# New order tables for all five engines of a two-layer linear-attention and SwiGLU kernel

## Chip, core and metric

The kernel runs on one core of one Trainium2 chip. The metric is device time in microseconds (us) of one execution. A core has TensorE (PE in the profile; PEld is its weight load), VectorE (DVE), ScalarE (ACT), GpSimd (POOL) and SyncE (SP), each with an instruction stream of its own; here SP issues every DMA.

## The reference

x is 2048 x 512 in float32. The same weights are used in both layers.

```python
def _A_ref(x, wqkv, wo):           # linear attention, H = 32 heads of 16
    q, k, v = ...                  # x @ wqkv, split by head
    phi = lambda t: jnp.where(t > 0, t + 1, jnp.exp(t)) + 1e-6
    pq, pk = phi(q), phi(k)
    kv = jnp.einsum("bhsd,bhse->bhde", pk, v)
    z = jnp.einsum("bhsd->bhd", pk)
    num = jnp.einsum("bhqd,bhde->bhqe", pq, kv)
    den = jnp.einsum("bhqd,bhd->bhq", pq, z)[..., None] + 1e-6
    return ... @ wo                # (num / den), heads joined

def _B_ref(x, w1, w3, w2):         # F = 1792
    return (silu(x @ w1) * (x @ w3)) @ w2

x = x + _A_ref(_layernorm(x), A_wqkv, A_wo)
x = x + _B_ref(_layernorm(x), B_w1, B_w3, B_w2)
x = x + _A_ref(_layernorm(x), A_wqkv, A_wo)
x = x + _B_ref(_layernorm(x), B_w1, B_w3, B_w2)
```

## The kernel before, in words

**Numbers.** Every float32 operand of a product is split into two float16 parts, a high one and a low one (the rest). `mm` (L878) makes each product as three matmuls (high by high, low by high, high by low; `PASSES`), each accumulating in a bank of PSUM.

**Attention.** The 2048 rows are 16 tiles of 128. Per tile t, `ln_moments` (L840, L841, VectorE) makes mean and variance; `ln_scale` makes the scale and the offset with four small GpSimd instructions: L848, the power of -1/2 (L849), L851, L852. `normalise` (L855, ScalarE) writes the normalised row. For a key tile, `keys_turn` makes the high part (L790 on ScalarE or L792 on GpSimd) and the low part (L1497, VectorE or GpSimd), and SP transposes both by DMA (L1498; L870 for the first three tiles). Then TensorE makes pk, the key product of 12 matmuls of 512 columns. phi of it is ScalarE's L1228 to L1230 and VectorE's L1239, and its parts are L1306 (ScalarE) and L1321 (VectorE). The sums over rows for the denominators are matmuls into pz (L1261) or adds on GpSimd (L1312). The Gram product gt takes 12 matmuls per key tile. The transposed tile is stored (`keep_transposed`, L1515) and read back for the queries (`load_query`, L1528). Weights for later come in meanwhile: x tiles L1977, attention weights L1982, blocks of w1 and w3 L893.

**MLP.** Rows go in four chunks of 512 (`mlp_rows`: transposes L1629 and L1637, store of the chunk L1641, reload L1813, 1792 KB each), the hidden width in seven groups of 256. Each group's first product has seven half-size products, P1 to P7, in place of eight. They go into three PSUM banks, ba, bb and bc. bb is copied to SBUF by ScalarE (L1692), and VectorE adds ba and bc (L1695), after which the next product may overwrite the bank. silu is L1647, times the second product L1648, and the parts of the hidden rows are L1651 and L1653. The second product goes into po: `mlp_out` (L1739), or at some places `mlp_out_plain` (L1759). `mlp_add` adds po to the rows in SBUF (L1788 on VectorE, then L1808 and L1809 on GpSimd; L1775 on VectorE after the plain form), and `store_row` (L1769) sends rows to the output. Prepared groups of weights are kept in DRAM (stores L1111, fetches L1120).

**What sets the order.** Each engine runs its own instructions strictly in its stream's order, and an instruction waits there for what it needs from others. The function `arrange` at the end of the trace takes, for each engine, a string of the table `ORDER`: the traced instructions' numbers in the order in which they are to stand. It makes each instruction depend on the one that the string puts ahead of it, without any semaphore (`tc.add_manual_dep(..., NoSync)`), so the tables fix all five streams and nothing else does. A number is the instruction's place in the order in which the program text issues it. SP's stream has a second rule: its DMAs take eight semaphores in turn, so a DMA waits for the landing of the one eight places ahead.

The program's own text already has an order of work (the strings `KEYS`, `FIRST`, `TURN`, `HOOKS`), and a table of which engine does each movable operation (`ENGINES`). The tables come from a planner outside the file that gives every instruction a duration; only its results, the strings, are in the kernel.

Of the kernel before, what the change touches and what calls it, by code (L numbers as in the profile page):

```python
# [73 lines left out]
        "0-56 59-61 57-58 62-64 71-82 65-67 85-87 68-70 94-108 91-93 83-84 109-113 117-119 88-90 "  # L74
        "114-116 123-134 137-139 149-160 120-122 143-145 140-142 135-136 161-172 146-148 184-186 "
        "175-177 181-183 207-212 173-174 187-198 201-203 178-180 204-206 199-200 213-226 230-232 "
        "239-250 227-229 233-235 265 251-252 266 259-261 256-258 284-286 253-255 236-238 267-280 "
        "262-264 281-283 290-292 287-289 293-304 313-315 305-306 319-330 316-318 310-312 331-332 "
        "339-341 345-356 342-344 307-309 333-335 368-370 336-338 371-382 365-367 357-358 392-394 "
        "359-361 389-391 395-396 418-420 397-408 383-385 409-411 421 362-364 386-388 422-424 "  # L80
        "412-417 431-433 428-430 446 425-427 437-439 434-436 443-445 440-442 447-570 583-594 "
        "571-582 595-762 775-786 763-774 787-883 908-913 920-925 884-895 932-943 896-907 926-931 "
        "914-919 956-973 980-991 1016-1027 944-949 1124 974-979 1125 950-955 992-1003 1028-1033 "
        "1126 1034-1039 1127 1064-1069 1128-1130 1004-1009 1131-1135 1010-1015 1136-1137 1140 "
        "1138-1139 1388 1100-1105 1389-1390 1106-1111 1391 1144 1392 1145 1393 1052-1057 1394 "
        "1146-1147 1395-1396 1141-1142 1397 1040-1045 1398-1402 1070-1075 1403 1046-1051 "
        "1408-1409 1404-1406 1410-1411 1407 1143 1058-1063 1232 1412 1233-1235 1076-1081 1413 "
        "1082-1087 1112-1123 1172-1177 1414-1415 1088-1099 1236 1416 1237-1249 1178-1183 1252 "
        "1250 1253-1254 1417-1418 1251 1419 1428 1148-1153 1208-1213 1160-1171 1154-1159 "
        "1420-1423 1340-1343 1424 1220-1225 1214-1219 1280-1285 1255 1184-1189 1425 1190-1195 "  # L90
        "1316-1321 1426 1344-1345 1322-1327 1286-1291 1346 1348 1196-1201 1226-1231 1347 "
        "1349-1354 1356 1202-1207 1355 1357-1362 1429 1427 1432 1430 1433-1435 1363 1256-1261 "
        "1431 1436 1262-1267 1437 1444 1438 1268-1273 1439-1443 1445-1446 1274-1279 1447-1459 "
        "1292-1297 1328-1333 1298-1303 1460-1471 1304-1315 1496-1501 1334-1339 1520-1537 "
        "1502-1504 1538 1376-1381 1540-1542 1364-1369 1382-1387 1784 1370-1375 1785 1539 1543 "
        "1786 1508-1513 1628-1630 1505-1507 1631 1472-1477 1514-1519 1787-1788 1478-1483 "
        "1568-1573 1789-1791 1632 1636 1574-1579 1484-1495 1633-1635 1637-1643 1648 1644-1647 "
        "1649 1792-1793 1604-1609 1794-1798 1556-1561 1544-1555 1562-1567 1610-1615 1799-1805 "
        "1736 1808 1616-1621 1809 1580-1585 1737-1738 1586-1591 1676-1681 1739 1650 1622-1627 "
        "1810 1651 1811 1592-1603 1740 1806-1807 1741-1757 1812 1652-1657 1682-1687 1813-1816 "  # L100
        "1658-1663 1817-1821 1712-1717 1822 1664-1669 1823 1670-1675 1824-1830 1718-1723 1832 "
        "1831 1833-1835 1688-1693 1836-1837 1840 1838-1839 1841-1843 1694-1699 1844-1845 1848 "
        "1846 1758-1759 1847 1849-1851 1724-1729 1852-1854 1856-1861 1855 1700-1705 1862-1867 "
        "1892-1897 1706-1711 1730-1735 1916-1917 1920-1921 1924-1925 1918-1919 1760-1765 "
        "1772-1777 1928 1778-1783 1930 1929 1766-1771 1922-1923 1931-1932 1926-1927 1934 "
        "1868-1873 1898-1903 1874-1879 1904-1909 2021-2022 1910-1915 1933 1936 1935 1880-1891 "
        "1961-1972 2023-2026 1937-1942 1997-2002 2029-2030 2027-2028 2031-2032 2035-2036 "
        "2039-2040 2003-2008 2037 1949-1960 1973-1978 1943-1948 1979-1984 2038 2009-2014 "
        "2033-2034 1985-1990 2066-2071 2102-2107 2015-2020 2041 2138-2139 2134-2135 1991-1996 "
        "2126-2127 2072-2077 2136-2137 2042-2047 2128-2131 2140 2132-2133 2144-2146 2141 "  # L110
        "2108-2113 2054-2065 2048-2053 2114-2119 2142 2120-2125 2078-2083 2171-2172 2143 "
        "2173-2174 2234-2241 2185 2084-2089 2186 2175-2178 2187-2188 2196-2197 2192-2193 "
        "2179-2182 2189-2190 2194 2183-2184 2090-2101 2191 2195 2200-2201 2198-2199 2202-2209 "
        "2213-2214 2210-2211 2221 2159-2164 2147-2152 2217-2218 2153-2158 2219-2220 2165-2170 "
        "2222 2215-2216 2212 2223-2226 2229 2242-2245 2270-2275 2230-2233 2276-2281 2227-2228 "
        "2282-2287 2339-2340 2294-2295 2341-2343 2246-2251 2298-2299 2296-2297 2252-2257 "
        "2302-2305 2300-2301 2308 2312 2306-2307 2313 2258-2263 2288-2293 2310 2314 2344-2345 "
        "2264-2269 2309 2311 2399-2400 2375-2380 2315-2320 2381-2386 2327-2338 2321-2326 "
        "2401-2404 2411-2412 2346-2350 2405-2410 2387-2392 2413 2444-2449 2414-2418 2504-2505 "
        "2351-2362 2480-2485 2393-2398 2419 2363-2374 2486-2491 2450-2455 2506-2511 2516-2518 "  # L120
        "2512-2515 2519-2524 2432-2437 2420-2425 2438-2443 2549-2552 2563-2564 2570-2571 "
        "2426-2431 2572-2573 2584-2585 2553-2554 2591-2592 2456-2461 2593-2594 2605-2606 "
        "2462-2467 2555-2556 2565-2566 2574-2577 2586-2587 2557-2562 2567 2492-2497 2568-2569 "
        "2582-2583 2595-2596 2578-2581 2588-2590 2597-2598 2468-2473 2599-2600 2498-2503 "
        "2672-2673 2474-2479 2601-2602 2607 2603-2604 2609-2611 2525-2530 2612-2621 2648 "
        "2537-2548 2622-2623 2531-2536 2649-2653 2608 2674-2675 2660-2665 2654-2659 2624-2629 "
        "2666-2671 2676-2677 2630-2635 2680-2683 2678-2679 2684-2686 2688 2690 2687 2717-2722 "
        "2689 2777-2778 2636-2641 2691 2723-2727 2642-2647 2753-2758 2692 2779-2782 2693-2698 "
        "2785-2788 2728 2789-2790 2705-2710 2797 2711-2716 2795 2791 2783-2784 2792-2793 2796 "
# [1963 lines left out]
```

## Time and profile before

| what | us |
|---|---|
| three runs: median (lowest to highest) | 1154.07 (1153.33 to 1154.54) |
| the profiled run, whole | 1151.51 |
| its span, from the first to the last instruction | 1149.8 |
| TensorE busy in it | 1139.5 |
| VectorE, ScalarE, GpSimd busy | 822.0, 628.8, 405.8 |
| first key product of layer 0 starts | 11.93 |

The profiled execution is one run of its own; 1.7 us of its time lie outside the span. The stages can be told by the lines on TensorE: keys of layer 0 up to about 105 us, queries and output of the attention to 188, the first MLP to about 590 while the keys of layer 1 begin at about 575, the second attention to 755, the second MLP to the end.

A row of the timeline reads: start, length, engine, line, operation, output and inputs, count; in brackets how long the engine was idle ahead of it, and what released it. Rows of the same operation that follow one another are drawn together. In the list of waits a row has the waiting engine and line, what released it, then the total in us, the number of times and the longest. Matmuls are pipelined, so a row of x12 is longer by one matmul's passage than its twelve issues.

### The profile page before, as it was taken

How to read it: one execution, taken by the hardware profiler on the slowest of the kernel's cores; microseconds unless marked ns; L12 is line 12 of the kernel's file. 1: busy time of each engine (PE TensorE's matmuls, PEld its weight loads, DVE VectorE, ACT ScalarE, POOL GpSimd, SP SyncE). 2: the span in 40 equal slices, each digit the busy share in tenths (PEclk: the TensorE clock that was granted, in tenths of full speed). 3: DMA queues.
4: the chain of work that ended last, by engine and by line, in shares of the span. 5: the costliest groups of instructions: out<-in, count | busy, mean ns of one | idle time of the engine just before them, and what ended most of it. 6: DMA issues, size and time to landing. Idle time of an engine off the chain costs nothing.

```text
span 1149.8 us, 21802 instructions
## 1 busy us (share of the span) xinstructions
PE 1139.5 (99%) x8862; PEld 864.0 (75%) x8862; DVE 822.0 (71%) x1401; ACT 628.8 (55%) x1078; POOL 405.8 (35%) x472
## 2 busy tenths in 40 slices
PE   8999999999999999999999999999999999999998
PEld 3445445888888888888854454478888888888887
DVE  6888888977878986778774467847866676556533
ACT  6587878866544554334457644776554434343422
POOL 4533688411101312212568615771153110303111
PEclk9999999999999999999999999999999999999999
DMA  9975666875854221111314715674253440022001
GB/s 277 316 231 201 183 171 129 229 170 180 242 203 182 99 84 65 65 65 66 92 32 128 216 41 122 120 172 93 77 134 116 169 174 1 28 80 101 1 19 56
DMA packets 163397, 147.43 MB, mean 128 GB/s; under 512 B 129632, under 2 KB 138976, under 8 KB 158688
## 3 DMA queue, kind: packets, MB, share of 16 engines
q1 hardware_dynamic: 163296, 146.04, 44.3%
q8 instruction: 69, 1.13, 0.4%
q14 instruction: 32, 0.26, 0.1%
HBM read 72.48 MB, written 42.07 MB: 100 GB/s over the span
## 4 chain that ended last, share of the span: by engine, by line
PE 94%; POOL 3%; DMA 1%; DVE 1%; ACT 1%; issue 0%; SPq 0%; POOLq 0%
PE bb L878 25%; PE po L1739 18%; PE bc L878 13%; PE pq L878 7%; PE po L878 7%; PE ba L878 6%; PE gt L878 6%; PE pk L878 5%; PE po L1759 4%; DMA arena<-arena 1%; DMA arena<-in_A_x_dram 1%; POOL arena L1312 0%; PE kv L878 0%; PE pm L878 0%; PE pz L1261 0%; POOL rs_all L849 0%
## 5 line engine op out<-in xcount | busy, mean ns | idle before, releaser
L878 PEld LDWEIGHTS <-arena 128*128 128x128 f16 x6360 | 617.8, 98 | 242.5 <-DMA arena<-arena 6.6
L878 PE MATMUL bb<-arena 128*128 128x256 f16 x2688 | 348.7, 273 | 0.1
L1739 PE MATMUL po<-arena 128*128 128x256 f16 x1932 | 266.7, 273 | 0.0
L1692 ACT ACTIVATE arena<-bb 128x512 f32<-128x512 f32 x196 | 115.8, 593 | 226.0 <-PE bb L878 186.5
L1739 PEld LDWEIGHTS <-arena 128*128 128x128 f16 x1932 | 189.0, 98 | 22.3
L878 PE MATMUL bc<-arena 128*128 128x256 f16 x1344 | 178.9, 273 | 0.0
L1695 DVE TENSOR_TENSOR arena<-arena,bc 128x512 f32<-128x512 f32 x112 | 76.7, 685 | 102.5 <-PE bc L878 56.6
L1653 DVE TENSOR_TENSOR arena<-arena 128x512 f16<-128x512 f32 (+1 forms) x90 | 104.4, 1162 | 32.1 <-ACT arena L1651 32.1
L1647 ACT ACTIVATE arena<-arena,scalars 128x512 f32<-128x512 f32 (+1 forms) x112 | 74.5, 666 | 96.2 <-DVE arena L1695 87.0
L1651 ACT ACTIVATE arena<-arena 128x512 f16<-128x512 f32 (+1 forms) x112 | 98.9, 886 | 33.5 <-DVE arena L1666 13.1
L1788 DVE SCALAR_TENSOR_TENSOR arena<-po,scalars,arena 128x256 f32<-128x256 f32 (+1 forms) x170 | 94.6, 584 | 27.5 <-PE po L1739 18.9
L1648 DVE SCALAR_TENSOR_TENSOR arena<-arena,scalars 128x512 f32<-128x512 f32 (+1 forms) x112 | 80.9, 723 | 39.4 <-ACT arena L1647 38.0
L878 PE MATMUL ba<-arena 128*128 128x256 f16 x672 | 92.1, 273 | 0.0
L878 PE MATMUL pk<-arena 128*128 128x512 f16 x384 | 87.8, 379 | 3.3 <-DMA arena<-arena 3.3
L878 PE MATMUL gt<-arena 128*128 128x512 f16 x384 | 88.9, 379 | 0.8 <-ACT arena L1306 0.6
L878 PE MATMUL pq<-arena 128*128 128x512 f16 x384 | 86.6, 379 | 0.0
L878 PE MATMUL po<-arena 128*128 128x512 f16 x384 | 86.5, 379 | 0.0
L1808 POOL TENSOR_TENSOR arena<-arena 128x512 f32<-128x512 f32 x25 | 34.1, 1366 | 114.7 <-DVE arena L1788 114.7
L1653 POOL TENSOR_TENSOR arena<-arena 128x512 f16<-128x512 f32 x22 | 27.0, 1225 | 124.2 <-ACT arena L1651 84.5
L1809 POOL TENSOR_TENSOR arena<-arena 128x512 f32<-128x512 f32 x25 | 37.0, 1479 | 84.0 <-DVE arena L1788 83.9
L1759 PE MATMUL po<-arena 128*128 128x256 f16 x480 | 64.8, 273 | 0.0
L855 ACT ACTIVATE arena<-arena,nb_all,rs_all 128x512 f32<-128x512 f32 x64 | 51.0, 805 | 17.4 <-POOL nb_all L852 14.4
(163 smaller groups left out, 1286.1 us busy)
## 6 DMA issues: line engine op xcount, KB each, us to landing
arena<-xb_d SPq DMA_DIRECT2D x12, 1792.0 KB, 7.7
xb_d<-arena SPq DMA_DIRECT2D x8, 1792.0 KB, 7.5
xt_d<-arena SPq DMA_DIRECT2D x32, 256.0 KB, 3.3
arena<-xt_d SPq DMA_DIRECT2D x32, 256.0 KB, 3.1
arena<-in_B_w_dram SPq DMA_DIRECT2D x8, 896.0 KB, 6.6
arena<-in_B_w_dram SPq DMA_DIRECT2D x28, 256.0 KB, 3.1
w_d<-arena SPq DMA_DIRECT2D x4, 1792.0 KB, 9.5
arena<-w_d SPq DMA_DIRECT2D x4, 1792.0 KB, 7.4
```

What stands on the lines that cost most here:

```text
L855: nc.scalar.activation(dst, x_sb[:, t, :], AF.Identity, scale=rs_all[:, t : t + 1], bias=nb_all[:, t : t + 1],)
L878: nc.tensor.matmul(dst, lhs(a, k), rhs(b, k), start=first and k == 0 and i == 0, stop=last and k == n - 1 and i == len(PASSES) - 1, skip_g ...
L1647: nc.scalar.activation(t, gate, AF.Silu, scale=info["u1"])
L1648: nc.vector.scalar_tensor_tensor(t, up, info["hid"], t, OP.mult, OP.mult)
L1651: nc.scalar.activation(hs[:, 0, lo:hi], t[:, lo:hi], AF.Copy)
L1653: engine.tensor_tensor(hs[:, 1, lo:hi], t[:, lo:hi], hs[:, 0, lo:hi], OP.subtract)
L1692: nc.scalar.activation(dst, bank_, AF.Copy)
L1695: nc.vector.tensor_tensor(dst, dst, bank_, OP.add)
L1739: nc.tensor.matmul(po[:, i * HALF : (i + 1) * HALF], hs[:, a, qx, cs], w2[:, b, qw, :], start=g == ends[0] and i + a + b == 0, stop=g == e ...
L1759: nc.tensor.matmul(acc[n][:, half * HALF : (half + 1) * HALF], hs[:, a, qx, cs], w2_a21[g][:, b] if (i, half) == (0, 1) else w2[:, b, i + ...
L1788: nc.vector.scalar_tensor_tensor(dst, src, cb, to, OP.mult, OP.add)
L1809: engine.tensor_tensor(x1, x1, u[:, 1:], OP.add)
```

## The change

Only the strings in `ORDER` differ; every other line is the same, though 16 lines lower, as the new strings take 16 lines more (L1769 of the kernel before is L1785 after). The words that come with it: all engines' tables are chosen anew, the planner gives each transfer more room, and it no longer keeps VectorE out of the time of GpSimd's power operation (L849).

In the same place as before stand 1840 of TensorE's 8845 numbers, 313 of VectorE's 1369, 319 of ScalarE's 1025, 181 of GpSimd's 470 and 75 of SP's 326. No number moves to another engine. The largest moves are 93 places forward and 89 back on TensorE, 45 and 155 on VectorE, 42 and 51 on ScalarE, 15 and 24 on GpSimd, 31 and 18 on SP. The beginnings and ends of the strings:

```diff
     "PE": (
-        "0-56 59-61 57-58 62-64 71-82 65-67 85-87 68-70 94-108 91-93 83-84 109-113 117-119 88-90 "
+        "0-56 59-61 57-58 62-64 71-82 65-70 94-108 123-134 88-90 85-87 83-84 109-113 135-136 "
...
-        "8833-8837 8832 8838-8844"
+        "8827-8831 8833 8832 8834-8844"
     "DVE": (
-        "1 6-15 17 16 18 5 19 28 21 20 29 26 30 27 22-25 33 36 34 37 31 43-44 35 45 38-40 52-53 "
+        "1 6-7 5 8-10 12 11 13-15 17 16 18-19 28 20 29 21 33 22-24 34 25-26 30 27 31 36-37 43 45 "
...
-        "1348 1345 1336 1346 1353-1354 1356 1347 1355 1357 1359 1351 1350 1358 1352 1360-1368"
+        "1362 1361 1363-1366 1368 1367"
     "Activation": (
-        "0-13 15 14 17 16 19 18 21-23 20 25 24 26 28 27 30 29 32 34 33 35-36 38 31 41 39-40 42-43 "
+        "0-12 14 13 15 17 19-20 16 18 21 23 22 25 24 26 28 27 30 29 31-32 34 33 41 38 35-36 40 39 "
...
     "Pool": (
-        "6-7 9 8 10 13 11 0 12 14-15 1-2 16-17 19 18 20-21 24 22 28 26 23 31-32 25 27 29-30 33-35 "
+        "6-7 9 8 10-15 0-2 16-17 19 18 20 22 24 23 21 28 26 25 30 27 29 31-35 37 39-40 45 36 42 "
...
     "SP": (
-        "0-7 30 21 8 11-12 9 22 10 26 19 18 25 24 23 20 17 29 13 28 27 38 15 41 31 33 32 39 34-35 "
-        "44 47 37 40 46 42 45 48 36 54 43 53 50 49 51-52 55 63 56-57 14 59 58 61 60 62 16 64 66 "
+        "0-2 4 3 5-6 21 7-8 11 10 9 12 26 19 29 18 30 20 22-24 17 27 45 28 25 13 31 33 32 44 41 "
+        "34-36 46 37 14 39 15 43 42 53 38 81 40 48 47 54 16 51 63 58 49 52 66 50 56-57 55 59 "
...
-        "276 275 277-284 297 286-289 285 291 290 292-294 302 299 296 298 295 301 304 300 307 "
-        "305-306 309-311 308 303 312 314 313 315-325"
+        "272 274-279 281-284 280 285-290 297 292 291 294 293 299 296 302 300 295 303 298 307 "
+        "305-306 309-310 308 311-312 314-315 313 301 316-320 304 321-325"
```

In SP's strings, the numbers 8, 9, 18, 23 and 27 are the transposes of key tiles 0 to 4 of layer 0; 30 is the load of x tile 9; 19, 20, 24 and 28 are stores of transposed tiles; 22, 25 and 29 are blocks of w1. On TensorE, 33-44, 45-56, 71-82, 97-108 and 123-134 are the key products pk of tiles 0 to 4; 65-70, 85-87 and 94-96 are parts of gt of the earlier tiles. The numbers 1367 and 1368 of VectorE are the last two adds of L1775, and 324 and 325 of SP the last two stores of rows (L1769): 324 sends the rows that 1367 writes, 325 those of 1368.

692 rows, old and new, of the table ORDER are left out of this document.

## The prediction

> **What bounds the kernel now.** I read the page's first part, then the list of what PE waited for, then busy time by stretch. The clock stayed at full speed ("clock 1.000"), so it drops out.
>
> ```profile
> span 1149.8 us, 21802 instructions
> ...
> PE 1139.5 (99%) x8862; PEld 864.0 (75%) x8862; DVE 822.0 (71%) x1401; ACT 628.8 (55%) x1078; POOL 405.8 (35%) x472
> ```
> ```profile
> core 0: 1149.8 us, clock 1.000
> ```
> ```profile
> PE pk L878 <- DMA arena<-arena: 3.3, 4, 1.4
> PE pm_k L739 <- POOL arena masks.py:199: 1.2, 1, 1.2
> PE warm L2006 <- DVE ones L663: 1.1, 1, 1.1
> PE gt L878 <- ACT arena L1306: 0.6, 1, 0.6
> PE gt L878 <- DVE arena L1321: 0.2, 1, 0.2
> ```
> ```profile
> 0.00:27.50 27.50, 22.14 (x90) 8.89 (x90) 17.13 (x44) 17.43 (x27) 12.72 (x35) 1.00 0.98 268
> ...
> 188.00:575.00 387.00, 386.93 (x3512) 343.50 (x3511) 313.29 (x527) 204.20 (x343) 99.61 (x96) 1.00 0.44 133
> ...
> 595.00:625.00 30.00, 28.98 (x134) 12.93 (x133) 14.28 (x26) 20.07 (x32) 27.51 (x45) 1.00 0.37 88
> ...
> 755.00:1135.00 380.00, 380.00 (x3462) 338.54 (x3460) 227.72 (x347) 174.39 (x273) 90.99 (x86) 1.00 0.28 87
> 1135.00:1150.00 15.00, 10.99 (x101) 9.60 (x99) 6.19 (x8) 2.37 (x4) 1.16 (x1) 1.00 0.19 71
> ```
>
> The columns behind the span are busy time (and instructions) of PE, PEld, DVE, ACT and POOL, then clock, DMA share and GB/s. PE is busy 386.93 of 387 us and 380 of 380 us in the two MLPs. Nothing that another engine does there can be seen in the time unless it makes PE wait. All that an order can win is in three places: the start (the list's waits for pk's transposes and for gt), one wait at the layer turn (1.02 us missing in 595:625), and the end (the last 15 us, with 10.99 of PE). The matmuls before the first keys (warm, pm_k) only fill time.
>
> **The change part by part.** No instruction is added or removed. PE keeps 8845 matmuls, VectorE 1369, ScalarE 1026, GpSimd 470 instructions and SP 326 DMAs; only their order on each engine differs. So the sum holds only pauses of PE gained and lost, and the end.
>
> *The start.* PE's pauses behind the first key products, and the DMA that ends them:
>
> ```profile
> 11.93 5.60 PE L878 MATMUL pk<-arena 128*128 128x512 f16 x24 [0.43 <-DMA arena<-arena]
> ...
> 18.13 0.59 PE L878 MATMUL gt<-arena 128*128 128x512 f16 x2 [0.61 <-ACT arena L1306]
> ...
> 21.82 2.76 PE L878 MATMUL pk<-arena 128*128 128x512 f16 x12 [1.45 <-DMA arena<-arena]
> ...
> 27.55 2.76 PE L878 MATMUL pk<-arena 128*128 128x512 f16 x12 [0.37 <-DMA arena<-arena]
> ```
> ```profile
> 22.30 5.20 DMA arena<-arena
> ```
>
> The transposes of tiles 0 to 3 are released behind a saturated DMA (share 0.98, 268 GB/s). SP's new table sends the x tile of position 30 (256 KB) behind the third transpose instead of ahead of the first, so every one of the first three has 256 KB less in front of it. At 268 GB/s that is 0.98 us, the upper end; I take 0.57 us for tile 2, because the tile also overlaps computing and its share of that time is not all on the path. In before, tile 3's transpose stood in SP's queue behind a store that waited for tile 2's transpose (it issued at 22.30, just after tile 2's products began at 21.82). In the new table that store (position 24) stands behind the transpose (23), which only needs the low part of tile 3, whose VectorE instruction is also earlier. Tile 4's cast, low part and transpose come some five to seven places earlier, and its products follow tile 3's directly. What is late next is tile 4: I expect it about 2.5 us behind tile 3, where 2.76 us of tile 3's products cover it. **Gain 0.55 us**: the 1.45 us pause shrinks by 0.57, and the 0.37 us pause stays in about its size, as three gt matmuls (85-87) less stand in front of tile 3's products. Bounds: both shrink fully, 0.57 + 0.37 = 0.94; or tile 4's cover is short by as much as one saturated 256 KB transfer, 0.98, which loses 0.98 - 0.55, about 0.4.
>
> *The power operation.* The old plan kept VectorE and GpSimd's power operation (L849) apart; the new one lets them lie together. Where they met anyway:
>
> ```profile
> 18.11 0.75 DVE L1321 SCALAR_TENSOR_TENSOR arena<-arena,scalars 128x512 f16<-128x512 f32 x1 [0.19 <-ACT arena L1306]
> 18.12 0.55 POOL L849 TENSOR_TENSOR rs_all<-ve,minus_half 128x1 f32<-128x1 f32 x1
> ```
> ```profile
> L1321 DVE SCALAR_TENSOR_TENSOR arena<-arena,scalars x32: 734/752/1693, 18.1 to 660.0; 128x512 f16<-128x512 f32 x32
> ```
> ```profile
> L849 POOL TENSOR_TENSOR rs_all<-ve,minus_half x29: 542/556/1095, 5.0 to 640.9; 128x1 f32<-128x1 f32 x28, 128x4 f32<-128x4 f32 x1
> ```
>
> VectorE's instruction took 0.75 us, its median (min/median/max 734/752/1693), through the whole 0.55 us of the power beside it. The power itself reaches 1095 ns at worst, so if either pays, it is GpSimd. Cost 0; bounds 0 and the 0.54 us more that GpSimd paid at worst, once on the way to a key. The Trainium skill (GPSIMD Engine Reference, section 1, Specifications) says that GpSimd's SBUF interfaces are shared with VectorE, with contention for VectorE instructions that have two SBUF inputs; L1321 is one, and this trace shows no time lost on VectorE's side. By that rule VectorE could be held for each power's time; that is the fifth case below.
>
> *The layer turn.* The wait is for tile 9's transpose, and GpSimd made it late:
>
> ```profile
> 617.57 1.27 POOL L1312 TENSOR_TENSOR arena<-arena 128x512 f32<-128x512 f32 x1
> 618.79 0.55 POOL L849 TENSOR_TENSOR rs_all<-ve,minus_half 128x1 f32<-128x1 f32 x1
> ...
> 619.84 1.16 POOL L1497 TENSOR_TENSOR arena<-arena 128x512 f16<-128x512 f32 x1
> ```
> ```profile
> 621.68 1.46 PE L878 MATMUL gt<-arena 128*128 128x512 f16 x6
> 624.16 2.76 PE L878 MATMUL pk<-arena 128*128 128x512 f16 x12 [1.02 <-DMA arena<-arena]
> ```
> ```profile
> 621.03 3.09 DMA arena<-arena
> ```
>
> GpSimd is busy 27.51 of 30 us there. The key's low part (L1497) sits behind an add (L1312, 1.27) of the denominators' sums, which has no early consumer. The new GpSimd table puts low parts ahead of these adds. The transpose at 621.03 starts as the low part ends (619.84 + 1.16 = 621.00). One L1312 out of its way makes it 1.27 us earlier; more than one goes by over the stretch, and walking the new order with these durations lands tile 9 at about 619.3. PE's six gt matmuls issue 0.216 us apart (1.46 = 5 x 0.216 + 0.38), so PE was free at 621.68 + 6 x 0.216 = 622.98 and lost 1.18 us. **Gain 1.2 us**; the pk of tiles 7 and 8 also move 1 to 2 us back in PE's order, which gives their transposes more time. Bounds: 1.2, or 0 if the adds that now come late hold the power operations of the next tiles instead (each 1.27).
>
> *The MLPs.* No pause of PE is there to win except 0.07 us (386.93 of 387); a copy that comes late costs. The leads are short:
>
> ```profile
> 420.55 0.60 ACT L1692 ACTIVATE arena<-bb 128x512 f32<-128x512 f32 x1 [1.49 <-PE bb L878]
> ```
> ```profile
> 421.22 0.82 PE L878 MATMUL bb<-arena 128*128 128x256 f16 x6
> ```
> ```profile
> L1692 ACT ACTIVATE arena<-bb 128x512 f32<-128x512 f32 x196 | 115.8, 593 | 226.0 <-PE bb L878 186.5
> ```
>
> This copy ended at 421.15 and the matmuls that overwrite its bank began at 421.22. There are 196 of them, but ScalarE stood idle 226 us ahead of them, mostly waiting for the matmuls themselves, so a copy normally starts when its product is done, in either order. The new order keeps each copy next to its product where I compared them (408 to 424). I take **0.1 us lost**; bounds 0.2 won, 1.5 lost (three copies, each behind another ScalarE instruction of about its own 0.6 us length).
>
> Of the transfers, one turns late: a 1792 KB reload (L1813), before issued at 316.50, now stands behind the fetch that waits for PE until 327.53.
>
> ```profile
> 296.95 5.91 SPq L1629 DMA_TRANSPOSE arena<-arena  x1
> ...
> 316.50 0.34 SPq L1813 DMA_DIRECT2D arena<-xb_d  x1
> 327.53 0.34 SPq L1120 DMA_DIRECT2D arena<-w_d  x1
> ```
> ```profile
> arena<-w_d SPq DMA_DIRECT2D x1, 1792.0 KB, 8.1
> w_d<-arena SPq DMA_DIRECT2D x1, 1792.0 KB, 12.0
> ```
>
> The second pair is what was issued between 320 and 345: two large transfers back to back landed after 8.1 and 12.0 us. So the reload lands at about 327.9 + 12 = 340; its products begin at 344.7. That covers it with over 4 us to spare, one more large transfer (12.0 - 8.1 = 3.9) included. The stores of weights that stood in front of transposes (behind one, a transpose held SP for 5.91 us at 296.95) move forward, which only adds room. Cost 0.
>
> *The end.*
>
> ```profile
> 1135.57 10.42 PE L1759 MATMUL po<-arena 128*128 128x256 f16 x94
> ```
> ```profile
> 1145.27 1.51 DVE L1775 SCALAR_TENSOR_TENSOR arena<-po,scalars,arena 128x512 f32<-128x512 f32 x2 [1.11 <-PE po L1759]
> ```
> ```profile
> 1146.05 0.33 SPq L1769 DMA_DIRECT2D out_dram<-arena  x1
> ```
> ```profile
> 1146.81 0.33 SPq L1769 DMA_DIRECT2D out_dram<-arena  x1
> ```
>
> PE ends at 1145.99. VectorE's last two adds are 0.75 us each: instruction 1367 runs at 1145.27, while PE still makes the last product, and 1368 at 1146.03, when it is done; each is stored as it ends. The new VectorE table ends "1368 1367": the add that needs PE's last product goes first and the one that was ready waits behind it. Both are then done at 1146.03 + 1.51 = 1147.54 instead of 1146.78. SP's table is unchanged there (324, 325), and 324 is the row of 1367; so both stores issue after 1147.54, the second one about 0.4 us behind the first (0.33 and the gap). Last issue 1147.57 + 0.4 = 1147.97 instead of 1146.81: **loss 1.15 us**. It lies behind PE, so nothing hides it. Bounds 0.75 (if the stores' gap does not count) and 1.3.
>
> *The sum.* -0.55 - 1.2 + 0.1 + 1.15 = -0.5. The profiled run took 1151.51 us (span 1149.8 and 1.7 around it), so its twin is 1151.0. The median of the runs shown is 1154.07, 2.56 above it, and I add the same: **1153.5 us**.
>
> **The rivals.** A measurement tells about 0.2% here, 2.3 us: faster is under 1151.8, slower over 1156.4.
> 1. *Only the end changes.* The start is bound by DMA whatever stands first, and late adds on GpSimd take the turn's gain back; the swap remains: 1154.07 + 1.15 = 1155.2. For it: DMA share 0.98 at the start. Against it: the turn's idle DMA (0.37).
> 2. *The pauses all go.* 0.61 + 0.19 + 1.45 + 0.37 at the start (the four behind the first key, 0.19 from the list's 0.2 row), 1.18 at the turn, less 1.15: 1154.07 - 2.65 = 1151.4. Against it: 256 KB less frees at most 0.98.
> 3. *Slower: bank copies miss.* In the MLPs the copies L1692 now lie behind other ScalarE instructions. Each miss costs PE about 0.6 - 0.07 = 0.5 us. It decides from (2.3 + 0.5) / 0.5, about six misses net; at eight of 196 the time is 1153.5 + 4.0 = 1157.5. For it: leads of 0.07 us, and 706 of ScalarE's 1025 table entries in another place. Against it: 226 us of idle time ahead of the copies.
> 4. *The order does not reach the chip or PE's cover hides it all*: no difference but noise, 1154.1. The end speaks against it, as nothing covers that; I count it with the first.
> 5. *VectorE is held by the power.* Four powers lie on the way to tiles 2 and 3; two on the path cost 2 x 0.55, and the start's gain is gone: 1153.5 + 1.1 + 0.55 = 1155.2.
>
> **How the numbers follow.** Forecast 0.52, cases 1 and 4 together 0.14, case 2 0.13, case 3 0.18, case 5 0.03. Faster comes from case 2 alone (0.13), slower from case 3 (0.18), within 0.2% from the rest (0.69). The range goes from 1151.0 (case 2 less its 0.4 us of unknown costs) to 1156.9: the forecast with every bound against it is 1153.5 + 0.55 + 0.4 + 1.2 + 1.4 = 1157.05, which is not likely all at once, and the part of case 3 beyond it is left out.
>
> **What would show it.** Right: tile 2's products start about 21.2, PE's wait for pk at the turn is gone from the list, and VectorE's last instruction ends about 1.5 us after PE's last matmul instead of 0.8. Wrong: a row "PE bb <- ACT L1692" or "PE <- DMA xb_d" in PE's list with over 1 us; a new pk wait between 28 and 105 us or between 600 and 669; an L1321 beside a power with over 1 us.

## The result, and the profile after

| | median of 22 runs (lowest to highest), us | span of the profiled run | TensorE busy |
|---|---|---|---|
| before | 1152.38 (1151.34 to 1154.54) | 1149.8 | 1139.5 |
| after | 1154.24 (1152.94 to 1156.09) | 1152.9 | 1140.2 |

The ratio after to before is 1.0014, 95% interval 1.0008 to 1.002: about 1.6 us slower (0.9 to 2.3). By the 0.2% bound this is no difference, as the prediction held likeliest, but it has the other sign: -0.5 us was forecast. The two profiled runs lie 3.1 us apart; that of before is one of its quickest, that of after one of its slower ones.

The page of after, and then what PE waited for (waiting line, releaser, total us, times, longest; L894 is L878 of before):

```profile
span 1152.9 us, 21848 instructions
...
PE 1140.2 (99%) x8862; PEld 863.9 (75%) x8862; DVE 815.7 (71%) x1401; ACT 631.0 (55%) x1078; POOL 401.7 (35%) x472
```
```profile
PE pk L894 <- DMA arena<-arena: 1.7, 3, 0.8
PE gt L894 <- DVE arena L1337: 1.5, 4, 0.8
PE gt L894 <- ACT arena L1322: 1.5, 1, 1.5
PE pm_k L755 <- POOL arena masks.py:199: 1.4, 1, 1.4
PE warm L2022 <- DVE ones L679: 1.1, 1, 1.1
```

The waits for transposes have halved (1.7 us for 3.3), as the change's words promise. In their place stand waits for gt, 3.0 us for 0.8: PE now waits for ScalarE and VectorE. By stretch (columns as in the prediction):

```profile
0.00:27.50 27.50, 22.81 (x95) 9.39 (x96) 19.09 (x49) 18.13 (x27) 13.17 (x37) 1.00 0.96 289
27.50:105.00 77.50, 76.14 (x356) 35.21 (x355) 63.29 (x122) 54.55 (x92) 28.23 (x58) 1.00 0.85 249
...
188.00:575.00 387.00, 387.00 (x3513) 343.40 (x3511) 314.53 (x528) 206.05 (x345) 98.30 (x95) 1.00 0.41 133
...
595.00:625.00 30.00, 28.86 (x133) 12.84 (x132) 15.94 (x28) 19.45 (x30) 28.38 (x44) 1.00 0.47 115
625.00:669.00 44.00, 43.66 (x201) 19.59 (x199) 17.82 (x24) 25.94 (x42) 23.19 (x29) 1.00 0.44 126
```

PE gains 0.67 us in the first 27.5 us (22.81 for 22.14) and loses more behind them: 76.14 of 77.50, for 77.45 before. The turn (595 to 669) has 1.48 us missing for 1.02. The MLP is as full as before.

To compare kernels whose matmuls stand in another order, I use one number: **PE's lateness**, the issue time of the matmul at which TensorE has so much work behind it, less that work, with 0.216 us counted for a matmul of 512 columns and 0.109 for another one (both rounded here), as the rows space them. A pause raises it, work doesn't. (The 96 matmuls of 128 columns are counted too high, half of them in each layer, so the column at 560 stands about 2.4 us too low and that at the end about 4.8; this is the same in every kernel.) "Missed issue" is what one pause adds to the lateness; the idle time in a row's brackets is about 0.17 us shorter, as it counts from the end of the matmul before. "Behind" is the span's time after PE's last matmul.

| kernel | at 60 us of work | at 560 | at the end | behind |
|---|---|---|---|---|
| before | 8.21 | 6.05 | 4.98 | 3.81 |
| after | 8.95 | 6.64 | 6.81 | 5.13 |
| b_tail | 7.90 | 5.81 | 4.78 | 5.14 |
| a_tail | 8.80 | 6.50 | 6.37 | 3.80 |
| b_start | 9.19 | 8.60 | 7.51 | 3.82 |
| b_turn | 8.45 | 6.35 | 6.24 | 3.81 |
| a_t8 | 9.93 | 7.77 | 8.22 | 5.13 |
| a_t68 | 10.05 | 7.75 | 8.48 | 5.13 |
| b_t9 | 8.45 | 6.41 | 8.50 | 3.82 |
| a_turn | 8.95 | 6.65 | 6.54 | 5.12 |
| a_pk | 10.92 | 8.62 | 8.82 | 5.14 |
| a_both | 9.52 | 7.23 | 7.58 | 5.14 |
| a_pow | 8.48 | 6.19 | 6.07 | 5.13 |
| b_turn_pe | 10.14 | 8.05 | 12.85 | 3.80 |
| b_pzv | 8.28 | 6.22 | 3.96 | 3.82 |
| a_pzv | 8.61 | 6.31 | 5.56 | 3.80 |
| a_phi0 | 7.79 | 5.89 | 5.99 | 5.14 |
| b_pzv_t3 | 8.16 | 6.11 | 3.84 | 3.81 |

The kernels named b_ are before with one or two edits, those named a_ are after with one or two. Two things show at once. The start scatters by 0.5 us and more from run to run in the same order (8.48 to 10.92 in the seven kernels that keep after's). The turn repeats: between 560 and 680 us of work the kernels with after's turn lose 0.94 us more than those with before's, and within each group the profiles agree to 0.1 us. Behind the turn up to 0.9 us more come in some profiles (0.3 in after's, most of it one wait of 0.26 us for a tile read back at 742 us; 0.05 in a_tail's). The end repeats to 0.02. And the pair in the first two rows splits into three: start +0.74 (8.95 - 8.21; 0.6 between the medians of the rows with an unchanged start, 8.37 and 8.95), the stretch from 560 on +1.24 (0.17 against -1.07; 0.94 of it is the turn), the end +1.32.

### The profile page after: what moved, and what is told of

Its sections match the earlier page's. It is cut to its first block, busy times and chain, and to the rows that moved or that the text cites. A ratio compares the mean times of both kernels' runs of the same rounds, so it can differ in the third digit from the quotient of the medians.

```text
span 1152.9 us, 21848 instructions
## 1 busy us (share of the span) xinstructions
PE 1140.2 (99%) x8862; PEld 863.9 (75%) x8862; DVE 815.7 (71%) x1401; ACT 631.0 (55%) x1078; POOL 401.7 (35%) x472
## 4 chain that ended last, share of the span: by engine, by line
PE 92%; POOL 3%; DMA 2%; ACT 1%; DVE 1%; issue 0%; SPq 0%; DVEq 0%; POOLq 0%
PE bb L894 25%; PE po L1755 18%; PE bc L894 13%; PE po L894 7%; PE pq L894 7%; PE ba L894 6%; PE po L1775 5%; PE gt L894 5%; PE pk L894 4%; DMA arena<-arena 1%; POOL rs_all L865 1%; DMA arena<-in_A_wqkv_dram 1%; POOL arena L1513 0%; PE kv L894 0%; PE pm L894 0%
## 5 line engine op out<-in xcount | busy, mean ns | idle before, releaser
L894 PEld LDWEIGHTS <-arena 128*128 128x128 f16 x6360 | 618.0, 98 | 243.9 <-issue 5.8
L894 PE MATMUL bb<-arena 128*128 128x256 f16 x2688 | 351.5, 273 | 0.0
L1755 PE MATMUL po<-arena 128*128 128x256 f16 x1932 | 271.6, 273 | 0.0
L894 PE MATMUL bc<-arena 128*128 128x256 f16 x1344 | 179.8, 273 | 0.0
L1669 DVE TENSOR_TENSOR arena<-arena 128x1280 f16<-128x1280 f32 (+1 forms) x90 | 105.1, 1172 | 33.8 <-ACT arena L1667 33.1
L1663 ACT ACTIVATE arena<-arena,scalars 128x512 f32<-128x512 f32 x112 | 74.6, 666 | 91.2 <-DVE arena L1711 79.3
L894 PE MATMUL gt<-arena 128*128 128x512 f16 x384 | 90.0, 379 | 3.2 <-DVE arena L1337 1.5
L894 PE MATMUL ba<-arena 128*128 128x256 f16 x672 | 92.7, 273 | 0.0
L894 PE MATMUL pk<-arena 128*128 128x512 f16 x384 | 87.5, 379 | 1.9 <-DMA arena<-arena 1.7
L894 PE MATMUL pq<-arena 128*128 128x512 f16 x384 | 86.6, 379 | 0.1
L894 PE MATMUL po<-arena 128*128 128x512 f16 x384 | 86.3, 379 | 0.0
L1824 POOL TENSOR_TENSOR arena<-arena 128x512 f32<-128x512 f32 x25 | 38.1, 1524 | 128.6 <-DVE arena L1804 128.6
L1775 PE MATMUL po<-arena 128*128 128x256 f16 x480 | 65.4, 273 | 0.0
L1679 POOL TENSOR_TENSOR arena<-arena 128x256 f32<-128x256 f32 x10 | 8.2, 825 | 142.2 <-DVE arena L1664 142.2
```

The costliest lines, as they stand in the source:

```text
L894: nc.tensor.matmul(dst, lhs(a, k), rhs(b, k), start=first and k == 0 and i == 0, stop=last and k == n - 1 and i == len(PASSES) - 1, skip_g ...
L1663: nc.scalar.activation(t, gate, AF.Silu, scale=info["u1"])
L1669: engine.tensor_tensor(hs[:, 1, lo:hi], t[:, lo:hi], hs[:, 0, lo:hi], OP.subtract)
L1755: nc.tensor.matmul(po[:, i * HALF : (i + 1) * HALF], hs[:, a, qx, cs], w2[:, b, qw, :], start=g == ends[0] and i + a + b == 0, stop=g == e ...
L1775: nc.tensor.matmul(acc[n][:, half * HALF : (half + 1) * HALF], hs[:, a, qx, cs], w2_a21[g][:, b] if (i, half) == (0, 1) else w2[:, b, i + ...
L1824: engine.tensor_tensor(x0, x0, u[:, 0::2], OP.add)
```

## The experiments

In the diffs a line is a cut of an engine's table. Line numbers of these kernels differ by a few tens, as the tables have other lengths; each is named by its operation.

**The end alone.** b_tail exchanges the two numbers in before; a_tail puts them back in after.

```diff
     "DVE": (                 b_tail
-  1360-1368
+  1360-1366 1368 1367
```

> The kernel before with only VectorE's last two numbers exchanged (1368 1367, as in the changed kernel). Theory: the two last adds follow PE's last matmul one after the other and both last stores follow them, so the end behind PE's last matmul grows from 3.8 us to about 5.0 us, and the median is 1.1 to 1.3 us above the kernel before. Rival: the exchange is the whole of the change's 1.9 us, and this kernel is 1.9 us above. Second rival: the stores' landing hides it, and the time is the same within 0.3 us.

> The changed kernel with VectorE's last two numbers back as before (1367 1368). Theory: 1.1 to 1.3 us are won back and about 0.6 us above the kernel before stays, which comes from PE's waits (in the profile of the changed kernel 1.83 us more of them than in that of before, which was a quick run). Rival (the end is all): the same time as before. Waits of PE for pk near 42 and 53 us and for gt near 610 us should be in its profile again, each of 0.5 to 1.2 us.

b_tail took 1.0009 (1.0000 to 1.0017) of before, 1.0 us; a_tail 1.0006 (0.9997 to 1.0015). "Behind" is 5.12 to 5.14 us in every kernel with 1368 ahead of 1367 and 3.80 to 3.82 in every one without: 1.32 us, whatever else is changed. In after, the two adds and the last two stores:

```profile
1147.86 1.41 DVE L1791 SCALAR_TENSOR_TENSOR arena<-po,scalars,arena 128x512 f32<-128x512 f32 x2 [1.21 <-PE po L1775]
```
```profile
1149.30 0.81 SPq L1785 DMA_DIRECT2D out_dram<-arena  x2
```

PE's last matmul ended at 1147.82; both adds follow it, and both stores follow them. The theory holds; the end isn't all of it. In a_tail's profile the waits near 53 and 610 us are there again, as expected; that near 42 us isn't.

**The start and the turn alone.** What before started in its first 105 us (b_start), or between 560 and 760 us (b_turn), in after's order on all engines, the rest in before's.

> The kernel before with the changed kernel's order for everything that before started in its first 105 us, on all engines; the rest in before's order. Theory: tile 2's and 3's products come 0.9 us earlier than before, then PE waits 0.7 us for tile 6's transpose near 42 us and 0.9 us for tile 8's near 53 us, so that PE is 0.5 to 0.9 us later than before from 60 us on, and the time is 0.5 to 0.9 us above. Rival: the two waits are noise of that one profiled run; then PE is 0.5 to 1.0 us ahead from 30 us to the end and the kernel is faster by that.

> The kernel before with the changed kernel's order only for what before started between 560 and 760 us. Theory: PE waits for gt (from VectorE's low part of phi) near 610 us by 0.8 to 1.2 us and again by 0.2 to 0.4 us two or three times up to 640 us, in place of one wait of 1.2 us for tile 9's transpose; the time is 0.6 to 1.1 us above before. Rival (as predicted): the wait for tile 9 goes and nothing takes its place, 1.2 us faster.

b_start: 1.0005 (0.9996 to 1.0014), b_turn: 1.0005 (0.9996 to 1.0014), about 0.6 us each, and neither is clear of zero by its runs. By its profile b_turn repeats after's five waits to 0.01 us (1.01 us of missed issue at 610.36, then 0.26, 0.35, 0.41 and 0.25), so the turn's loss is the order's, 1.0 us (from 560 to the end -0.11 against -1.07). What PE waited for between 600 and 660 us, first after, then b_turn:

```profile
PE gt L894 <- DVE arena L1337: 1.3, 3, 0.8
```
```profile
PE gt L859 <- DVE arena L1302: 1.3, 3, 0.9
```

b_start is 1.0 us later than before at 60, but the waits for tiles 6 and 8 aren't in its profile: it lost time at 19.7 and 27.9 us and in two waits at 108 and 223 us, behind the stretch that was exchanged. It does not test the start's mechanism.

**Tile 8 and tile 6.** After's waits at the start, and the chain of waits to the second of them:

```profile
18.84 0.59 PE L894 MATMUL gt<-arena 128*128 128x512 f16 x2 [1.48 <-ACT arena L1322]
...
21.41 2.76 PE L894 MATMUL pk<-arena 128*128 128x512 f16 x12 [0.32 <-DMA arena<-arena]
...
42.23 2.76 PE L894 MATMUL pk<-arena 128*128 128x512 f16 x12 [0.57 <-DMA arena<-arena]
...
53.12 2.76 PE L894 MATMUL pk<-arena 128*128 128x512 f16 x12 [0.79 <-DMA arena<-arena]
```
```profile
40.84 5.83 DMA arena<-in_A_wqkv_dram
...
46.73 6.34 DMA arena<-arena
```

Tile 2's pause is down to 0.32 us (1.45 before), tile 3's is gone. Tile 6's transpose lands at 42.2 (42.3 before), so PE, now 0.95 us ahead (lateness 7.26 for 8.21 at 30 us of work), waits for it. Tile 8's transpose was issued when the weight load eight places ahead of it had landed (40.84 + 5.83 = 46.67): SP's second rule, that a DMA waits for the one eight places ahead. Before issued that load at 34.54 us, ten places ahead of the transpose; the new table issues it at 40.84. Tile 8 is the wait that repeats: in all eight kernels with after's start in which its transpose isn't moved PE misses 0.66 to 1.42 us there, while tile 6 makes it wait in one of these eight, after. a_t8 moves that transpose forward, a_t68 also GpSimd's cast of tile 6:

```diff
     "SP": (                  a_t8, a_t68
-  43 42 53 38 81 40 48 47
+  43 42 48 53 38 81 40 47
     "Pool": (                a_t68
-  42 51 38 52 41 56 47 46 57 53 43 54 48 44
+  42 51 38 44 52 41 56 47 46 57 53 43 54 48
```

> The changed kernel with one SP number moved: 48, the transpose of tile 8, right behind 42 (tile 7's), ahead of the loads 53, 38, 81 and 40. In the changed kernel its data was ready at 44.43 and it issued at 46.73, as the DMA eight places ahead of it (an attention weight) landed only at 46.67. Theory: issued about 44.5, it lands near 50, and PE's wait of 0.95 us near 53 us goes; PE is up to 0.95 us earlier from 60 us on. Rival (the tile's low part or DMA's own load sets it): it lands within 1 us of 53 as before and the wait stays.

> As the last one, and GpSimd's cast of tile 6 (number 44) ahead of the four power operations and eight small operations that stood before it (its input was ready at 32.94, it ran at 35.53). Theory: tile 6's transpose issues about 2 us earlier and lands near 40, so PE's wait of 0.74 us near 42 us goes as well, and PE is up to 1.7 us earlier from 60 us on than in the changed kernel. Rival: tile 7 or 8, whose scales now come later on GpSimd, makes a new wait of the same size, and nothing is won against the kernel with 48 moved alone.

Both are slower than after: 1.0032 (1.0019 to 1.0044) and 1.0025 (1.0016 to 1.0034) of before. In a_t8 the wait at 53 us is gone, so the cause of that wait was right, and a new one of the same size stands 4 us later, with another of 0.55 us at 68. The chain of waits to the one at 57.62:

```profile
49.74 5.28 DMA arena<-in_A_wqkv_dram
...
55.04 1.87 DVE parts L716 x3
56.91 0.67 DVE arena L1317
...
57.62 0.38 PE pz L1257
```

The loads that the transpose had passed came later; VectorE takes the largest values of one of them (L716), and phi's low part stood behind that in VectorE's order. In a_t68 both waits are gone, others come at 58 and 68 us, and the pause near 19 us was so long that the clock fell (below). At the start DMA is nearly full (share 0.96, then 0.85 in the rows above); a place given to one transfer is taken from the next that somebody waits for.

**Tile 9 at the turn.** b_t9 is the prediction's reason for the turn, taken alone in before.

```diff
     "Pool": (                b_t9
-  297 290 293 295 305 291 296
+  297 291 290 293 295 305 296
```

> The kernel before with one GpSimd number moved: 291, the low part of tile 9 of layer 1, ahead of the add 290 and the power 293. It is the prediction's reason for the turn taken alone. Theory of the prediction: tile 9 lands 1.7 us earlier, its wait of 1.19 us goes, and nothing takes its place: 1.2 us faster than before. Rival (GpSimd has no slack): the add and the power come 1.2 us later, and a wait for gt or pk of 0.5 us or more appears within the next 20 us.

Tile 9's wait went, as predicted. And then:

```profile
628.79 2.48 PE L859 MATMUL gt<-arena 128*128 128x512 f16 x7 [2.27 <-DVE arena L1302]
```

PE waited 2.27 us for phi's low part, since the add and the power now came later (the power at 620.59 us for 618.79, and behind it ScalarE's normalising and phi): 1.0020 (1.0011 to 1.0029), 2.3 us slower. In the profile 1.7 us of the loss are a slower clock behind this pause (last section). The rival holds: on GpSimd what is brought forward pushes the rest back.

**What holds the wait of after at 610 us.** Rows of after, from four engines:

```profile
605.01 0.69 ACT L1244 ACTIVATE arena<-pk,scalars 128x512 f32<-128x512 f32 x1 [2.08 <-POOL arena L1328]
```
```profile
606.59 1.27 POOL L1328 TENSOR_TENSOR arena<-arena 128x512 f32<-128x512 f32 x1
```
```profile
606.91 1.49 DVE L1255 SCALAR_TENSOR_TENSOR arena<-arena 128x512 f32<-128x512 f32 x1 [3.06 <-ACT arena L1246]
...
609.20 1.40 DVE L1337 SCALAR_TENSOR_TENSOR arena<-arena,scalars 128x512 f16<-128x512 f32 x1 [0.19 <-ACT arena L1322]
```
```profile
610.65 2.32 PE L894 MATMUL gt<-arena 128*128 128x512 f16 x10 [0.84 <-DVE arena L1337]
```

ScalarE's phi (605.01) waits 2.08 us for one of the adds, whose input buffer it is to overwrite. VectorE's phi sum takes 1.49 us beside the next add, where 0.69 is its median. I first suspected the add (a_turn), then the later key product (a_pk), then the pair (a_both), and by itself the overlap on VectorE (a_pow):

```diff
     "Pool": (                a_turn, a_both
-  265 282 274 271 263 276
+  265 263 282 274 271 276
     "PE": (                  a_pk, a_both
-  4538-4540 4517-4519 4544-4555
+  4544-4555 4538-4540 4517-4519
     "Pool": (                a_pow
-  280 270 281 277
+  280 281 270 277
```

> The changed kernel with one GpSimd number moved: 263, the add into the denominators' sum whose input buffer ScalarE waits to overwrite (until 605.01), from behind 271 to behind 265. Theory (the add holds ScalarE's next phi, and adds of GpSimd beside VectorE's two-input operations stretch these from 0.69 to 1.49 us): ScalarE's phi starts about 1.2 us earlier, the wait of 1.01 us for gt near 610 us goes or falls under 0.3 us. Rival (GpSimd's throughput bounds the turn): the wait at 610 goes, but those near 617, 634 and 640 us grow by the same sum, and PE's end is where it was within 0.3 us.

> The changed kernel with one group of TensorE moved: the key product of 12 matmuls that began at 602.06 (numbers 4544 to 4555) six matmuls (1.3 us) earlier, where the kernel before had it within 0.1 us. Its tile had landed at 600.85. The last run moved an add of GpSimd and left the wait of 1.0 us at 610.66 as it was, so that was not the cause. Theory now: phi of this product needs 5.8 us from its last matmul to its low part, and the new TensorE table put the product 1.2 us later without moving its gt; so this edit takes the wait of 1.0 us near 610 us away (under 0.2 us left). Rival (GpSimd's chain sets the low part): the wait stays over 0.7 us.

> The changed kernel with both single moves of the turn made at once: TensorE's key product 4544 to 4555 six matmuls earlier, and GpSimd's add 263 behind 265. Either alone left the wait of 1.0 us near 610 us: with the add moved, ScalarE's phi waited for the product till 604.92; with the product moved, it waited for the add as long after the product as before. Theory (both end within 0.1 us of one another, and either holds phi): phi starts 1 us or more earlier and the wait near 610 us falls under 0.4 us; what is won goes over to the next waits near 617 us. Rival (a third cause, the stretched VectorE operations alone): the wait stays over 0.7 us.

> The changed kernel with one GpSimd pair exchanged: the power of number 281 (607.82) ahead of the add 270 (606.59). VectorE's phi sum at 606.91 took 1.49 us beside the add, 0.69 is its median. Theory: VectorE's operations with two SBUF inputs are held for as long as a wide add of GpSimd runs beside them, and not by a power; the phi sum takes 0.7 us here and PE's wait near 610 us falls from 1.0 us by 0.3 to 0.9. Rival (the power holds VectorE): the phi sum takes 1.2 us or more beside the power, and the wait stays.

a_turn and a_pk each left the wait (1.00 and 0.91 us of missed issue). ScalarE's row of each shows why, first a_turn, then a_pk:

```profile
604.92 0.69 ACT L1224 ACTIVATE arena<-pk,scalars 128x512 f32<-128x512 f32 x1 [1.99 <-PE pk L874]
```
```profile
607.00 0.69 ACT L1224 ACTIVATE arena<-pk,scalars 128x512 f32<-128x512 f32 x1 [2.09 <-POOL arena L1308]
```

With the add out of the way the product ends the same idle time (1.99 for 2.08 us); with the product out of the way the add does. The releaser that a row names is only the last of several. In a_both the wait at 610 is gone, and the next one near 617 grew from 0.26 to 1.18 us. a_pow, by another way, does the same (gone, and 1.19 us at 616.4). What PE waited for in them between 600 and 660 us, a_both and a_pow alike:

```profile
PE gt L874 <- ACT arena L1302: 1.0, 1, 1.0
PE gt L874 <- DVE arena L1317: 0.5, 2, 0.3
```

Between 560 and 625 us of work after loses 2.0 us, a_both 2.1 and a_pow 1.9. In a_pow phi's sum took 0.69 us for 1.49 (row in the last section), and its low part, for 1.40:

```profile
607.95 0.89 DVE L1317 SCALAR_TENSOR_TENSOR arena<-arena,scalars 128x512 f16<-128x512 f32 x1 [0.19 <-ACT arena L1302]
```

So the wait at 610 goes by an earlier phi, which takes both moves, or by unstretched steps of phi on VectorE, and curing it won nothing: the times are 1.0017 (1.0007 to 1.0027) and 1.0012 (1.0003 to 1.0020) of before. My expectations for a_turn and a_pk were wrong.

> The kernel before with only TensorE's order changed, and only for what before started between 560 and 760 us: the changed kernel's order there. All other engines have before's order. Theory (TensorE's later key products at the turn cost the wait for gt): a wait of 0.4 to 1.2 us for gt near 610 us appears, although GpSimd's, VectorE's and ScalarE's orders are before's. Rival (GpSimd's order makes it): no wait for gt near 610 us, and the wait for tile 9 shrinks, as its product stands later.

b_turn_pe, TensorE's new order at the turn with all other engines as before, took 1.0054 (1.0039 to 1.0068), 6.2 us more, with 0.8 to 1.3 us of missed issue for gt at 607, 619, 631 and 644 us and three more waits of 0.5 to 1.5 us between 683 and 745. TensorE's new order alone makes the waits, as expected, and more of them than with the other four tables, which fit it.

**GpSimd's load.** One add of the denominators' sum, that of tile 5, goes to VectorE in before (b_pzv) and in after with the end put back (a_pzv):

```diff
-            "pz:PPPPPPPPPPPVVPPP ..."
+            "pz:PPPPPVPPPPPVVPPP ..."      # 290 leaves the GpSimd table
     "DVE": (                 b_pzv (numbers counted with the new one)
-  878 859 866 863 864
+  878 859 866 862 863 864
```

> The kernel before with one add of the denominators' sum of layer 1 (tile 5, GpSimd at 617.57, 1.27 us) made by VectorE in an idle time near 614 us. Theory (at the turn GpSimd's throughput sets PE's waits, so an order alone wins nothing): the wait of 1.19 us for tile 9 falls under 0.3 us and no new wait over 0.3 us comes behind it; 0.9 to 1.2 us faster than before. Rival: the chain of phi (ScalarE, VectorE) takes its place as in the run with the low part moved, and the sum of waits between 600 and 660 us stays above 1 us.

> The changed kernel with the add of tile 5 into layer 1's denominators moved from GpSimd to VectorE (near 614 us) and VectorE's last two numbers back as before. Theory (GpSimd's throughput sets the turn in both orders): PE's waits from 610 to 660 us, 2.3 us in the changed kernel, fall by 0.8 us or more; with the end's 1.3 us won back the kernel is within 0.5 us of before. Rival (in the new order the waits come from the order of phi's steps, not from GpSimd's load): the waits stay over 2 us.

b_pzv: 0.9991 (0.9982 to 0.9999), 1.0 us faster, and the turn is full. Its stretch 595 to 625, and the moved add:

```profile
595.00:625.00 30.00, 30.00 (x140) 13.49 (x139) 16.23 (x28) 21.27 (x34) 27.42 (x45) 1.00 0.40 93
```
```profile
614.33 0.69 DVE L1293 TENSOR_TENSOR arena<-arena 128x512 f32<-128x512 f32 x1 [1.89 <-POOL arena L1293]
```

0.69 us on VectorE, in idle time, for 1.27 us on GpSimd: tile 9's wait is gone and nothing took its place (560 to the end -2.26 for -1.07). In after's order the same move takes only part: the waits at 634 and 640 us go, those at 610 to 618 (1.62 us together), which stand before the moved add, stay. That is 0.7 us of 2.3, short of the 0.8 expected: waits ahead of the moved add cannot gain by it, and they are the larger part. With the end's 1.3 us a_pzv is level with before: 0.9998 (0.9990 to 1.0007).

**The first pause, and the best version.**

```diff
     "DVE": (                 a_phi0
-  37 43 45 35 38
+  37 35 43 45 38
     "SP": (                  b_pzv_t3 (with b_pzv's edit)
-  18 25 24 23 20
+  18 25 23 24 20
```

> The changed kernel with one VectorE number moved: 35, the phi sum of tile 0, ahead of 43 and 45, the statistics of tiles 5 and 6, of which the first waits for its x tile's load. Theory of two parts: PE's pause for tile 0's gt near 19 us (1.1 to 2.3 us in six profiles of this order, 0.6 to 1.0 in before's) falls to 1.0 us or less; and it wins nothing at 60 us, as the waits for tiles 6 and 8 set PE there (PE's time less its work stays within 0.3 us of the changed kernel's). Rival: the pause's 0.7 us stay won to the end and the kernel is 0.7 us faster than the changed one.

> The kernel before with the add of tile 5 on VectorE (which alone was 1.2 us faster than before) and SP's number 23, the transpose of tile 3, ahead of the store 24 that waits for tile 2's transpose; this is the one step of the new start that needs no load moved. Theory: tile 3's transpose issues 1.3 us earlier and PE's pause of 0.2 to 0.5 us for it goes, but tile 6 (landed 0.15 us ahead of its product in before) takes the most of it back; 1.2 to 1.6 us faster than before. Rival: the store, now behind, delays the next transfers and a new wait of 0.3 us or more between 28 and 60 us takes all of it back or more.

a_phi0 is inconclusive: the pause near 19 us is 1.33 us of missed issue, inside the range of the other runs of that order, and PE is 1.2 us earlier at 60 us in this one profile, but the runs took 1.0013 (1.0005 to 1.0022), the same as after. b_pzv_t3 is the fastest kernel of the study, 0.9984 (0.9974 to 0.9995), 1.8 us under before: in its profile tile 3's pause is gone and tile 6's comes to 0.19 us. How much of that belongs to the second edit is not clear, as b_pzv's interval holds it.

## Why the prediction was wrong, point by point

1. **What bounds the kernel**: right. The MLPs stayed full, and nearly all that changed lies in the three places named. (ScalarE's table has 1025 numbers; the prediction says 1026 in one place.)
2. **The start, gain 0.55.** The transposes did what was said and more: tile 2's landed 0.41 us earlier (21.36 for 21.77; 0.57 was taken), tile 3's 1.9 and tile 4's 5.4 us earlier, and at 30 us of work PE was 0.95 us ahead. The step that failed is "what is late next is tile 4". Tile 4 was in time; next were tile 6, whose landing the new order did not move, and tile 8, held by the DMA eight places ahead of it, a weight load that the new table issues 6.3 us later than the old. The prediction names no tile behind tile 4 and puts no price on them. At 60 us the start is 0.74 us behind in the pair of profiles. That tile 8's wait is the order's is shown; that it alone makes the start's loss isn't, since a_t8 took the wait away and won nothing.
3. **The power operation, cost 0**: right. In after two powers run under the whole of this VectorE instruction, and it takes its 0.75 us:

```profile
32.27 0.75 DVE L1337 SCALAR_TENSOR_TENSOR arena<-arena,scalars 128x512 f16<-128x512 f32 x1 [0.79 <-ACT arena L1322]
```
```profile
32.02 1.41 POOL L865 TENSOR_TENSOR rs_all<-ve,minus_half 128x1 f32<-128x1 f32 x2
```

4. **The layer turn, gain 1.2**: the main failure. It cost 0.94 us where 1.2 were to be won. Tile 9's transpose did move as reckoned (issued at 619.25, the 619.3 that the prediction calls its landing, for 621.03; it landed at 622.29, ahead of its product), and its wait went. "Which has no early consumer" was false: ScalarE's phi waits for the add, to overwrite its input. "Gives their transposes more time" was counted as good; the later products also start phi later, and their gt stood where it was. The lower bound (0) let late power operations take back the gain but cost nothing more, and left phi out. b_t9 shows that even the pure form of the step loses, and there through a power.
5. **The MLPs, 0.1 lost**: small, as said, but won: no wait for a bank, and the pause of 0.23 us at 196 went, 0.03 over the bound of 0.2 won. The moved reload landed at 341.7, for 340 reckoned, ahead of its use.
6. **The end, loss 1.15**: right, 1.32 measured, 0.02 over the bound given.
7. **The sum**: the profiles give 0.6 to 0.7 at the start, less 0.2 at 196, 0.9 to 1.2 from the turn on, and 1.3: 2.6 to 3.0 us. The runs say 1.6 (0.9 to 2.3). The rest is not settled; single profiles of the start scatter by more than that. That the time forecast, 1153.5, lies 0.7 us from the measured 1154.24 is luck: its base was the median of three runs, 1154.07, which 22 runs put at 1152.38. This 1.7 us hid most of the error of 2.1 us in the change (-0.5 for +1.6).

Of the rivals, none was it. By the change against before, the first (only the end changes) and the fifth came nearest, both at +1.1 us; the first's words "late adds on GpSimd take the turn's gain back" have the right engine. The fourth's time, 1154.1, is nearest only by the high base. What the third and fifth describe did not happen.

## What to carry to other kernels

Where one engine is full and its feeders wait for one another, a gain in front of a wait is worth only the slack up to the next one: walk the next four or five consumers before counting it. An instruction's consumers include the next writer of each buffer it reads. When single moves only shift a wait, count the load of the engine behind it and take work off it; one 1.27 us add moved to an idle engine won 1.0 us, where five new tables lost 1.6.

## What the runs showed of the hardware

**GpSimd's wide adds and VectorE exclude one another.** In after, VectorE's two-input phi sum started at 606.91, 0.32 us into an add of GpSimd that ended at 607.86, and took 1.49 us instead of 0.69. In a_pow it started first, and the add beside it paid instead (two adds in 3.31 us, for 1.27 each):

```profile
606.47 0.69 DVE L1235 SCALAR_TENSOR_TENSOR arena<-arena 128x512 f32<-128x512 f32 x1 [3.06 <-ACT arena L1226]
```
```profile
606.65 3.31 POOL L1308 TENSOR_TENSOR arena<-arena 128x512 f32<-128x512 f32 x2
```

So whichever starts later waits for the other. In after's trace all eight phi sums (L1255) that started during a wide GpSimd operation ended 0.54 to 0.55 us after it; none of the 17 instructions of L1609, which read one input from the product po in PSUM, took longer beside such an operation (0.74 to 0.75 us). A power of one column beside it costs VectorE nothing, so by these rows the old plan's exclusion named the wrong GpSimd operation. The Trainium skill (GPSIMD Engine Reference, section 1, Specifications) has contention between GpSimd and VectorE instructions with two SBUF inputs; these rows agree for wide operands and show it as waiting for the whole operation.

**A pause of 2 us costs 1.7 us more.** Behind b_t9's wait of 2.27 us eight matmuls came 0.43 us apart instead of 0.216, and the granted clock of that stretch is 0.80; in a_t68 a pause of 2.12 us did the same at the start, clock 0.62 (the eighth column):

```profile
625.00:633.50 8.50, 6.23 (x22) 2.38 (x20) 6.22 (x9) 7.00 (x12) 7.79 (x12) 0.80 0.52 154
```
```profile
20.00:24.50 4.50, 4.31 (x13) 1.60 (x12) 3.06 (x6) 3.39 (x6) 0.00 (x0) 0.62 1.08 373
```

a_pk had it as well behind 2.0 us; the longest pause without it was a_turn's, 1.9 us. 8 x 0.21 = 1.7 us. The new order's first pause (1.1 to 2.3 us of missed issue, 0.6 to 1.0 in before's) lies near that edge, which may be part of its scatter. The Trainium skill (TensorE: Matmul & The Clock Gate, "What's actually happening") gives an idle window of about 3.4 us; here 2.0 to 2.3 us sufficed.
